# Moving one transpose and one store to other queues, reordering the early loads, and folding in smaller steps in a matmul-bound kernel

## The chip, the cores and the metric

One core of one Trainium2 chip. The time is device microseconds of one execution, the median over runs; all runs told here are of the state fast. The profile's span is some 1.8 us shorter than the time of the same run (567.7 beside 569.45 before the change).

## The reference, cut to what matters

```python
B, N, C = 4, 5824, 256
qn = q / (norm(q, axis=1) + 1e-6);  kn = k / (norm(k, axis=1) + 1e-6)
a  = softmax(kn^T @ qn / tau)              # 256 x 256 per batch
x  = (v @ a).reshape(B * N, C)
out = ((x @ w1) * (x @ w2)) @ w3 @ w_out   # d_ff = 1024
```

The kernel never forms x. It folds the softmax into w1 and w2 per batch (`Wf`), multiplies v transposed (`vT`) by it, and forms W = w3 @ w_out once.

## The kernel before

Three places matter. The first folds, 256 columns of each half at a time, with the eviction cut in two:

```python
def first_folds():
    sum_mm(0)
    for c1 in range(CT): quarter_mm(0, c1, 0)      # 2 matmuls of 256 columns
    sum_mm(1)
    for c1 in range(CT): quarter_mm(0, c1, 1)      # then Wf by ScalarE (c1 = 0) and VectorE
```

The start of the main loop: w3 is loaded right behind v pieces 1 and 2; piece 1 of v is transposed on TensorE, piece 2 by DMA behind the transposes of w3; loads for the next batch follow. `hold` is a one-element GpSimd copy that reads what a transpose wrote, so GpSimd issues nothing further until it has landed:

```python
load_piece("v", 0, 1); load_piece("v", 0, 2)
nc.gpsimd.dma_start(out=wout_sb, ...); nc.gpsimd.dma_start(out=w3_bf, in_=w3r)
# ... (cut)
at(7.0, 0.5, lambda: transpose_half_on_pe(0, 1, 0, True))
at(8.0, 0.5, lambda: transpose_half_on_pe(0, 1, 1, False))
at(15.0, 0.0, transpose_w3)
at(15.0, 0.0, lambda: transpose_piece(0, 2))
for jt in range(FT):
    at(27.5 + 1.2 * jt, 0.87, lambda jt=jt: w_unit(jt))     # the products w3 @ w_out
moves = [("qk", 1, 0, 29.0), ("v", 0, 3, 30.0), ("v", 0, 4, 30.5), ("qk", 1, 1, 44.0), ...]
```

The last stores: two of 64 left rows each on SyncE, one of 128 rows on ScalarE's queue:

```python
for m in (b - 1, b):
    nc.sync.dma_start(out=out[m * N + NT * P : (m + 1) * N, :], in_=o2[k : k + LEFT, :])
```

Of the kernel before, what the change touches and what calls it, by code (L numbers as in the profile page):

```python
# [12 lines left out]
F32 = DT.float32  # L13
BF16 = DT.bfloat16

P = 128
# [9 lines left out]
def kernel(  # L26
# [113 lines left out]
    def transpose_half_on_pe(n, pi, h, on_act):  # L140
        if pi == 0 and h == 0:
            new_vT(n)
        t = pieces["v", n, pi]
        i0 = 4 * h
        pe_transpose(
            vTs[n][0][:, pi * PIECE + i0 : pi * PIECE + i0 + 4, :, :].rearrange("p i c t -> p (i c) t"),
            [t[:, i0 + i, ct * P : (ct + 1) * P] for i in range(4) for ct in range(CT)],
            "out", on_act,
        )
# [93 lines left out]
    def soft_units(n):  # L243
# [133 lines left out]
            for c2 in range(CT):  # L377
                fold_mm((w, c1, h * 512, (h + 1) * 512), c2, tag, i % 2 == 0 or (n == 0 and i == 7))

        def quarter_mm(lo, c1, c2):  # L380

            if c2 == 0:
                tag = "ab" if lo == 0 else "out"
                st[lo, c1] = psum.tile(
                    [P, 2, 256], F32, tag=tag, name=f"quarter_{lo}_{c1}", bufs={"ab": 4, "out": 3}[tag]
                )
            m = st[lo, c1]
            for w in range(2):
                nc.tensor.matmul(  # L389
                    m[:, w, :], lhsT=st["e"][:, c2, c1 * P : (c1 + 1) * P], rhs=w12[:, c2, w, lo : lo + 256],  # L390
                    start=(c2 == 0 and w == 0), stop=(c2 == CT - 1 and w == 1), skip_group_check=True,
                )
            if c2 == CT - 1:
                for o in (0, P) if lo == 0 else (slice(0, 256),):
                    cols = slice(o, o + P) if lo == 0 else o
                    dst, src = Wf[n][:, c1, :, lo : lo + 256][:, :, cols], m[:, :, cols]
                    if c1 == 0:
                        nc.scalar.activation(out=dst, in_=src, func=AF.Copy, scale=st["rs"][:, c1 : c1 + 1])  # L398
                    else:
                        nc.vector.tensor_scalar_mul(dst, src, st["rs"][:, c1 : c1 + 1])  # L400

        def first_folds():
            sum_mm(0)
            for c1 in range(CT):
                quarter_mm(0, c1, 0)
            sum_mm(1)
            for c1 in range(CT):
                quarter_mm(0, c1, 1)

        def second_quarter():  # L410
            for c1 in range(CT):
                for c2 in range(CT):
                    quarter_mm(256, c1, c2)

        if n == 0:
            return [k_first, k_row, q_first, scaled_first, first_folds, second_quarter, sum_start] + [lambda i=i: fold(i) for i in range(4, 8)]
# [24 lines left out]
    def at(t, cost, fn):  # L441
        seq[0] += 1
        agenda.append((t, seq[0], cost, fn))
# [22 lines left out]
    def hold(src):  # L466

        nc.gpsimd.tensor_copy(gate_t, src)  # L468
# [33 lines left out]
    def emit_out(b, c, j, ab, only=None):  # L502

        small = c == NCH - 1
        if small:
            lhs = [ab[:, :P]]
            if b % 2 == 1:
                lhs.append(lefts[b // 2][:, j, :, :].rearrange("p b t -> p (b t)")[:, P : P + 2 * LEFT])
        else:
            lhs = [ab[:, i * P : (i + 1) * P] for i in range(4)]  # L510
        if j == 0:
            out_tiles[b, c] = [
                psum.tile([P, 2, D], F32, tag="out", name=f"o_{b}_{c}_{h}", bufs=3)
                for h in range(len(lhs) if small else 2)
            ]
        tl = out_tiles[b, c]
        for s, lhsT in reversed(list(enumerate(lhs))) if small else enumerate(lhs):
            if only is not None and s != only:
                continue
            h, o = (s, 0) if small else divmod(s, 2)  # L520
            nc.tensor.matmul(  # L521
                tl[h][:, o, :], lhsT=lhsT, rhs=W_sb[:, j, :],
                start=(j == 0 and o == 0), stop=(j == FT - 1 and (small or o == 1)),
                skip_group_check=True,
            )
        clock[0] += len(lhs) * (D * MM_COL + MM_FIX)
        if j == FT - 1:
            o = work.tile([P, 4, D], F32, tag="o_sb", name=f"osb_{b}_{c}", bufs=3)
            rows = out[b * N : b * N + NT * P, :].rearrange("(p i) c -> p i c", i=NT)
            if small:  # L530
                if b % 2 == 1 and only != 0:
                    o2 = work.tile([P, D], F32, tag="kr", name=f"oleft_{b}", bufs=1)
                    nc.vector.tensor_copy(o2, tl[1][:, 0, :])
                    for m in (b - 1, b):
                        k = (m - b + 1) * LEFT
                        nc.sync.dma_start(out=out[m * N + NT * P : (m + 1) * N, :], in_=o2[k : k + LEFT, :])
                if only != 1:
                    nc.scalar.copy(o[:, 0, :], tl[0][:, 0, :])
                    other = nc.scalar if b == B - 1 else nc.sync
                    other.dma_start(out=rows[:, NT - 1, :], in_=o[:, 0, :])  # L540
            else:
                nc.scalar.copy(o[:, 0:2, :], tl[0])  # L542
                nc.vector.tensor_copy(o[:, 2:4, :], tl[1])  # L543
                nc.sync.dma_start(out=rows[:, 4 * c : 4 * c + 4, :], in_=o)
            if only is None:
                del out_tiles[b, c]
# [72 lines left out]
    load_part("v", 0, 0, half, PIECE)  # L619
    load_piece("v", 0, 1)  # L620
    load_piece("v", 0, 2)
    nc.gpsimd.dma_start(out=wout_sb, in_=moe_w_out.rearrange("(lh ll) c -> ll lh c", ll=P))
    nc.gpsimd.dma_start(out=w3_bf, in_=w3r)
    squares("k", 4, whole)
    for sl in (lo, hi):
        squares("q", 4, sl)
# [19 lines left out]
    def w_unit(jt):  # L646
# [10 lines left out]
        if jt == FT - 1:  # L657
            w_ready[0] = True

    def load_library():  # L660

        m = work.tile([P, 1], F32, tag="lib", name="lib", bufs=1)
        nc.gpsimd.partition_all_reduce(m, ones_f, P, ReduceOp.add)


    def make_agenda(b):
        agenda.clear()
        clock[0] = 0.0
        n = b + 1
        if b == 0:  # L670
            at(0.5, 0.87, soft0[5])
            for i in range(4):
                at((1.7, 2.6, 3.5, 3.9)[i], 0.43, soft0[7 + i])
            at(0.0, 0.0, load_library)
            at(4.6, 0.5, lambda: transpose_half_on_pe(0, 0, 1, False))
            at(7.0, 0.5, lambda: transpose_half_on_pe(0, 1, 0, True))
            at(8.0, 0.5, lambda: transpose_half_on_pe(0, 1, 1, False))
            at(15.0, 0.0, transpose_w3)
            at(15.0, 0.0, lambda: transpose_piece(0, 2))
            for jt in range(FT):  # L680
                at(27.5 + 1.2 * jt, 0.87, lambda jt=jt: w_unit(jt))
            moves = [("qk", 1, 0, 29.0), ("v", 0, 3, 30.0), ("v", 0, 4, 30.5), ("qk", 1, 1, 44.0), ("qk", 1, 2, 45.0)]
            moves += [("qk", 1, 3, 53.0), ("qk", 1, 4, 55.0), ("v", 0, 5, 61.0), ("qk", 1, 5, 73.0)]
            moves += [("v", 1, 0, 88.0), ("v", 1, 1, 98.0), ("v", 1, 2, 120.0), ("qk", 2, 0, 130.0)]
            t0, t1 = 54.0, 113.0
        else:
            moves = [("v", b, 3, 1.0), ("qk", n, 1, 10.0), ("qk", n, 2, 17.0), ("v", b, 4, 26.0), ("qk", n, 3, 38.0)]
            moves += [("v", b, 5, 46.0), ("qk", n, 4, 58.0), ("qk", n, 5, 66.0)]
            moves += [("v", n, 0, 76.0), ("v", n, 1, 86.0), ("v", n, 2, 96.0), ("qk", n + 1, 0, 108.0)]
            moves = [m for m in moves if m[1] < B]  # L690
            t0, t1 = 16.0, 98.0

        before = (0, 2) if b == 0 else None
        for nm, m, pi, t in moves:
            if before is not None and not (nm == "v" and before == (m, pi - 1) == (0, 3)):
                at(t, 0.0, lambda w=before: hold(vTs[w[0]][1][:1, 0, :1] if w[1] == NP_ - 1 else vTs[w[0]][0][:1, w[1] * PIECE, 0, :1]))
            at(t, 0.0, gate)
            if nm == "qk":
                at(t, 0.0, lambda m=m, pi=pi: load_qk(m, pi))
                before = None  # L700
            else:
                at(t, 0.0, lambda m=m, pi=pi: load_piece("v", m, pi))
                at(t + 4.0, 0.0, lambda m=m, pi=pi: transpose_piece(m, pi))
                before = (m, pi)
        if n == B:
            agenda.sort()
            return
        units = score_units(n)
        for i, (cst, fn) in enumerate(units):
            at(t0 + (t1 - t0) * i / len(units), cst, fn)  # L710
        soft = soft_units(n)
        for cst, t, fn in soft:
            at(t1 + 1.0 + t, cst, fn)
        agenda.sort()
# [55 lines left out]
```

## Time and profile before

| | before |
|---|---|
| median (lowest to highest) | 569.44 us (569.25 to 569.69) |
| first main matmul (a) starts | 37.27 us |
| last matmul starts | 563.39 us |
| gaps between matmuls after the first a | 1.13 us |
| last store lands / span ends | 566.76 / 567.68 us |

A gap is read from the starts of consecutive matmuls: what a step exceeds 0.216 us after 512 columns, 0.109 after 256, 0.082 after 192 and 0.055 after 128 by, where that is over 0.03 us. The three parts of the table, head, matmuls with their gaps, and tail, add up to the span.

### The profile page before, as it was taken

Reading aid. Unit: us, or ns where it says so; the run is one execution under the profiler, and the core shown is the slowest. Engines: PE = TensorE matmul, PEld = TensorE weight load, DVE = VectorE, ACT = ScalarE, POOL = GpSimd, SP = SyncE. Lnnn points to the kernel's source line nnn. Section 1 sums busy time; section 2 is a strip of 40 time slices with the busy share of each in tenths; the row PEclk is TensorE's granted clock in tenths of the full one; section 3 lists DMA queues with packets and bytes.
Section 4 is the critical chain, followed back from the end, with each engine's and each line's share of the span. In section 5 each row is a group of like instructions: output and inputs, shape, how many; then the busy total and the mean of one; then the engine's idle time right before and its main releaser. Section 6 shows DMA issues by size and latency. Waiting matters only on the chain.

```text
span 567.7 us, 10095 instructions
## 1 busy us (share of the span) xinstructions
PE 557.6 (98%) x3755; PEld 355.4 (63%) x3755; DVE 375.4 (66%) x581; ACT 338.7 (60%) x627; POOL 77.9 (14%) x163
## 2 busy tenths in 40 slices
PE   8799999999999999999999999999999999999997
PEld 5664566776656666666656566666655655665655
DVE  1047645888966577888766668787876665565564
ACT  1057536777766577777675567777765554454453
POOL 4260013120111111121210101030120000000000
PEclk9999999999999999999999999999999999999999
DMA  9999989978455796595661595765740325221011
GB/s 213 211 182 209 173 171 237 226 164 192 115 142 121 143 192 148 90 193 123 145 149 75 97 219 117 155 120 121 185 112 39 85 74 149 64 68 71 38 70 61
DMA packets 75104, 77.45 MB, mean 136 GB/s; under 512 B 54192, under 2 KB 58800, under 8 KB 75056
## 3 DMA queue, kind: packets, MB, share of 16 engines
q0 software_dynamic: 15760, 38.93, 39.3%
q1 hardware_dynamic: 59008, 37.23, 22.0%
q10 hardware_dynamic: 288, 0.66, 0.4%
q8 instruction: 29, 0.48, 0.3%
q14 instruction: 19, 0.16, 0.1%
HBM read 78.91 MB, written 23.86 MB: 181 GB/s over the span
## 4 chain that ended last, share of the span: by engine, by line
PE 93%; DMA 5%; ACT 1%; POOL 0%; issue 0%; DVE 0%; ACTq 0%; POOLq 0%
PE o L521 28%; PE b L476 28%; PE a L476 28%; PE G L192 5%; DMA k<-in_k_dram 5%; PE fold L363 2%; PE w L649 1%; ACT kr L283 0%; PE quarter L389 0%; POOL k L111 0%; POOL q L111 0%; PE sqk L225 0%; PE row L271 0%; ACT e L322 0%; ACT Wf L398 0%
## 5 line engine op out<-in xcount | busy, mean ns | idle before, releaser
L497 DVE TENSOR_TENSOR abs<-as,b 128x512 bf16<-128x512 bf16 x336 | 230.6, 687 | 143.9 <-ACT as L482 131.4
L482 ACT CAST as<-a 128x512 bf16<-128x512 f32 (+1 forms) x384 | 215.9, 562 | 170.4 <-DVE abs L497 84.7
L476 PEld LDWEIGHTS <-Wf 128*128 128x128 bf16 x1536 | 149.0, 98 | 102.3 <-ACT Wf L398 0.6
L476 PE MATMUL a<-vT,Wf 128*128 128x512 bf16 x704 | 209.6, 379 | 0.4 <-ACT Wf L398 0.4
L476 PE MATMUL b<-vT,Wf 128*128 128x512 bf16 x704 | 209.6, 379 | 0.0
L521 PE MATMUL o<-W_sb,abs 128*128 128x256 bf16 x1344 | 201.5, 273 | 0.0
L521 PEld LDWEIGHTS <-abs 128*128 128x128 bf16 x1344 | 131.2, 98 | 79.8 <-issue 0.2
L201 DVE TENSOR_TENSOR acc<-acc,sq 128x1024 f32<-128x1024 f32 x66 | 80.4, 1219 | 0.6 <-ACT sq L189 0.6
L192 PE MATMUL G<-k,q 128*128 128x256 bf16 x276 | 49.8, 273 | 0.0
L189 ACT ACTIVATE sq<-q 128x512 f32<-128x512 bf16 x66 | 41.8, 633 | 0.0
L189 ACT ACTIVATE sq<-k 128x512 f32<-128x512 bf16 x66 | 41.5, 629 | 0.0
L464 POOL COPY gate_t<-abs 1x1 bf16<-1x1 bf16 x39 | 10.5, 269 | 171.7 <-DVE abs L497 168.8
L543 DVE COPY osb<-o 128x512 f32<-128x512 f32 x44 | 30.1, 685 | 0.9 <-PE o L521 0.9
L192 PEld LDWEIGHTS <-q 128*128 128x128 bf16 x276 | 27.0, 98 | 3.1
L542 ACT COPY osb<-o 128x512 f32<-128x512 f32 x44 | 25.8, 586 | 4.1 <-PE o L521 2.1
L468 POOL COPY gate_t<-vT 1x1 bf16<-1x1 bf16 x16 | 3.1, 193 | 158.8 <-DMA vT<-v 158.8
L111 POOL DMA_DIRECT2D q<-in_q_dram x28 | 15.1, 540 | 12.5 <-DMA k<-in_k_dram 5.5
L370 ACT ACTIVATE Wf<-fold,rs 128x512 bf16<-128x512 f32 x15 | 10.3, 687 | 10.9 <-PE fold L363 8.7
L283 ACT ACTIVATE kr<-row 128x256 f32<-128x256 f32 x1 | 0.4, 383 | 26.1 <-PE row L271 26.1
L363 PE MATMUL fold<-w,e 128*128 128x512 bf16 x56 | 15.0, 379 | 0.0
L487 DVE TENSOR_TENSOR left<-as,b 128x192 bf16<-128x192 bf16 x32 | 11.3, 354 | 5.1 <-ACT as L482 2.7
L497 DVE TENSOR_TENSOR abq<-as,b 128x512 bf16<-128x512 bf16 x16 | 10.8, 686 | 5.0 <-ACT as L482 4.5
(98 smaller groups left out, 242.3 us busy)
## 6 DMA issues: line engine op xcount, KB each, us to landing
out_dram<-osb SPq DMA_DIRECT2D x44, 512.0 KB, 3.3
k<-in_k_dram POOLq DMA_DIRECT2D x19, 512.0 KB, 8.3
v<-in_v_dram POOLq DMA_DIRECT2D x19, 512.0 KB, 5.2
q<-in_q_dram POOLq DMA_DIRECT2D x18, 512.0 KB, 5.8
w_wout<-in_moe_w_dram POOLq DMA_DIRECT2D x1, 2048.0 KB, 22.7
k<-in_k_dram POOLq DMA_DIRECT2D x4, 320.0 KB, 8.8
v<-in_v_dram POOLq DMA_DIRECT2D x4, 320.0 KB, 4.9
q<-in_q_dram POOLq DMA_DIRECT2D x3, 320.0 KB, 4.1
```

What stands on the lines that cost most here:

```text
L111: nc.gpsimd.dma_start(out=pieces[nm, n, pi][:, lo:hi, :], in_=qk_main[nm, n][0][:, pi * PIECE + lo : pi * PIECE + hi, :])
L189: nc.scalar.activation(out=dst[:, :, part, :], in_=src[:, o : o + 2, :], func=AF.Square)
L192: nc.tensor.matmul(G[:, ct, :], lhsT=qt[:, i, ct * P : (ct + 1) * P], rhs=kt[:, i, :], start=(pr == 0 and part == 0 and ct == 0), stop=(pr ...
L201: nc.vector.tensor_add(accs[n], accs[n], sqs[0])
L363: nc.tensor.matmul(m, lhsT=st["e"][:, c2, c1 * P : (c1 + 1) * P], rhs=w12[:, c2, w, lo:hi], start=(c2 == 0), stop=(c2 == CT - 1),)
L476: nc.tensor.matmul(t[:, :n], lhsT=Wf[b][:, ct, w, j * P : (j + 1) * P], rhs=rhs_of(b, c, ct), start=(ct == 0), stop=(ct == CT - 1),)
L482: nc.scalar.copy(a_sb[:, :n], tiles[0][:, :n])
L487: nc.vector.tensor_mul(both, a_sb[:, :n], tiles[1][:, :n])
L497: nc.vector.tensor_mul(ab, a_sb, tiles[1])
L521: nc.tensor.matmul(tl[h][:, o, :], lhsT=lhsT, rhs=W_sb[:, j, :], start=(j == 0 and o == 0), stop=(j == FT - 1 and (small or o == 1)), skip ...
L542: nc.scalar.copy(o[:, 0:2, :], tl[0])
L543: nc.vector.tensor_copy(o[:, 2:4, :], tl[1])
```

## The change

Its intent: take sixteen transposes off TensorE, start the first fold's eviction sooner, keep the transfer queue free for what is needed first, and let the last two stores start side by side.

```diff
+            for c1 in range(CT):                      # first folds: 128 + 128 columns
+                for c2 in range(CT):
+                    columns_mm(P, P, c1, c2)
-                        nc.sync.dma_start(out=..., in_=o2[k : k + LEFT, :])
+                        eng = nc.gpsimd if m == B - 1 else nc.sync
+                        eng.dma_start(out=..., in_=o2[k : k + LEFT, :])
-    nc.gpsimd.dma_start(out=wout_sb, ...)             # behind the v loads
-    nc.gpsimd.dma_start(out=w3_bf, in_=w3r)
-            at(7.0, 0.5, lambda: transpose_half_on_pe(0, 1, 0, True))
-            at(8.0, 0.5, lambda: transpose_half_on_pe(0, 1, 1, False))
+            at(0.0, 0.0, lambda: transpose_piece(0, 2))
+            at(0.0, 0.0, lambda: transpose_piece(0, 1))
+            at(0.0, 0.0, lambda: hold(vTs[0][0][:1, PIECE, 0, :1]))
+            at(0.0, 0.0, load_w3)                     # the two loads above
-                at(27.5 + 1.2 * jt, 0.87, lambda jt=jt: w_unit(jt))
+                at(35.5 + 1.2 * jt, 0.87, lambda jt=jt: w_unit(jt))
-            moves = [("qk", 1, 0, 29.0), ("v", 0, 3, 30.0), ("v", 0, 4, 30.5), ("qk", 1, 1, 44.0), ...]
+            moves = [("qk", 1, 0, 35.0), ("v", 0, 3, 35.5), ("qk", 1, 1, 49.0), ..., ("v", 0, 4, 60.0), ...]
```

(Cut: the rest of the moves, renamings, and the first hold, which now waits for the last transpose of w3.)

More of the change, by code (lines that the diff above doesn't have):

```diff
@@ L378, in fold, with columns_mm @@
                 fold_mm((w, c1, h * 512, (h + 1) * 512), c2, tag, i % 2 == 0 or (n == 0 and i == 7))
-        def quarter_mm(lo, c1, c2):
+        def columns_mm(lo, width, c1, c2):
             if c2 == 0:
-                tag = "ab" if lo == 0 else "out"
+                tag = "ab" if lo < 256 else "out"
                 st[lo, c1] = psum.tile(
-                    [P, 2, 256], F32, tag=tag, name=f"quarter_{lo}_{c1}", bufs={"ab": 4, "out": 3}[tag]
+                    [P, 2, width], F32, tag=tag, name=f"columns_{lo}_{c1}", bufs={"ab": 4, "out": 3}[tag]
                 )
@@ L389, in quarter_mm @@
                 nc.tensor.matmul(
-                    m[:, w, :], lhsT=st["e"][:, c2, c1 * P : (c1 + 1) * P], rhs=w12[:, c2, w, lo : lo + 256],
+                    m[:, w, :], lhsT=st["e"][:, c2, c1 * P : (c1 + 1) * P], rhs=w12[:, c2, w, lo : lo + width],
                     start=(c2 == 0 and w == 0), stop=(c2 == CT - 1 and w == 1), skip_group_check=True,
@@ L393, in quarter_mm @@
             if c2 == CT - 1:
-                for o in (0, P) if lo == 0 else (slice(0, 256),):
-                    cols = slice(o, o + P) if lo == 0 else o
-                    dst, src = Wf[n][:, c1, :, lo : lo + 256][:, :, cols], m[:, :, cols]
-                    if c1 == 0:
-                        nc.scalar.activation(out=dst, in_=src, func=AF.Copy, scale=st["rs"][:, c1 : c1 + 1])
-                    else:
-                        nc.vector.tensor_scalar_mul(dst, src, st["rs"][:, c1 : c1 + 1])
+                dst = Wf[n][:, c1, :, lo : lo + width]
+                if c1 == 0:
+                    nc.scalar.activation(out=dst, in_=m, func=AF.Copy, scale=st["rs"][:, c1 : c1 + 1])
+                else:
+                    nc.vector.tensor_scalar_mul(dst, m, st["rs"][:, c1 : c1 + 1])
         def first_folds():
@@ L404, in first_folds @@
             for c1 in range(CT):
-                quarter_mm(0, c1, 0)
+                columns_mm(0, P, c1, 0)
             sum_mm(1)
             for c1 in range(CT):
-                quarter_mm(0, c1, 1)
+                columns_mm(0, P, c1, 1)
+            for c1 in range(CT):
+                for c2 in range(CT):
+                    columns_mm(P, P, c1, c2)
         def second_quarter():
@@ L412, in second_quarter @@
                 for c2 in range(CT):
-                    quarter_mm(256, c1, c2)
+                    columns_mm(256, 256, c1, c2)
         if n == 0:
@@ L535, in emit_out @@
                         k = (m - b + 1) * LEFT
-                        nc.sync.dma_start(out=out[m * N + NT * P : (m + 1) * N, :], in_=o2[k : k + LEFT, :])
+                        eng = nc.gpsimd if m == B - 1 else nc.sync
+                        eng.dma_start(out=out[m * N + NT * P : (m + 1) * N, :], in_=o2[k : k + LEFT, :])
                 if only != 1:
@@ L621 @@
     load_piece("v", 0, 2)
-    nc.gpsimd.dma_start(out=wout_sb, in_=moe_w_out.rearrange("(lh ll) c -> ll lh c", ll=P))
-    nc.gpsimd.dma_start(out=w3_bf, in_=w3r)
     squares("k", 4, whole)
@@ L658, in w_unit, with load_w3 @@
             w_ready[0] = True
+    def load_w3():
+        nc.gpsimd.dma_start(out=wout_sb, in_=moe_w_out.rearrange("(lh ll) c -> ll lh c", ll=P))
+        nc.gpsimd.dma_start(out=w3_bf, in_=w3r)
     def load_library():
@@ L675, in make_agenda @@
             at(4.6, 0.5, lambda: transpose_half_on_pe(0, 0, 1, False))
-            at(7.0, 0.5, lambda: transpose_half_on_pe(0, 1, 0, True))
-            at(8.0, 0.5, lambda: transpose_half_on_pe(0, 1, 1, False))
-            at(15.0, 0.0, transpose_w3)
-            at(15.0, 0.0, lambda: transpose_piece(0, 2))
+            at(0.0, 0.0, lambda: transpose_piece(0, 2))
+            at(0.0, 0.0, lambda: transpose_piece(0, 1))
+            at(0.0, 0.0, lambda: hold(vTs[0][0][:1, PIECE, 0, :1]))
+            at(0.0, 0.0, load_w3)
+            at(16.0, 0.0, transpose_w3)
             for jt in range(FT):
-                at(27.5 + 1.2 * jt, 0.87, lambda jt=jt: w_unit(jt))
-            moves = [("qk", 1, 0, 29.0), ("v", 0, 3, 30.0), ("v", 0, 4, 30.5), ("qk", 1, 1, 44.0), ("qk", 1, 2, 45.0)]
-            moves += [("qk", 1, 3, 53.0), ("qk", 1, 4, 55.0), ("v", 0, 5, 61.0), ("qk", 1, 5, 73.0)]
-            moves += [("v", 1, 0, 88.0), ("v", 1, 1, 98.0), ("v", 1, 2, 120.0), ("qk", 2, 0, 130.0)]
+                at(35.5 + 1.2 * jt, 0.87, lambda jt=jt: w_unit(jt))
+            moves = [("qk", 1, 0, 35.0), ("v", 0, 3, 35.5), ("qk", 1, 1, 49.0), ("qk", 1, 2, 51.0), ("qk", 1, 3, 55.0)]
+            moves += [("qk", 1, 4, 57.0), ("v", 0, 4, 60.0), ("qk", 1, 5, 80.0), ("v", 0, 5, 83.0)]
+            moves += [("v", 1, 0, 97.0), ("v", 1, 1, 106.0), ("v", 1, 2, 120.0), ("qk", 2, 0, 130.0)]
             t0, t1 = 54.0, 113.0
@@ L691, in make_agenda @@
             t0, t1 = 16.0, 98.0
-        before = (0, 2) if b == 0 else None
+        before = "w3" if b == 0 else None
         for nm, m, pi, t in moves:
             if before is not None and not (nm == "v" and before == (m, pi - 1) == (0, 3)):
-                at(t, 0.0, lambda w=before: hold(vTs[w[0]][1][:1, 0, :1] if w[1] == NP_ - 1 else vTs[w[0]][0][:1, w[1] * PIECE, 0, :1]))
+                at(t, 0.0, lambda w=before: hold(w3T[-1][:1, 1, FT - 1, :1] if w == "w3" else vTs[w[0]][1][:1, 0, :1] if w[1] == NP_ - 1 else vTs[w[0]][0][:1, w[1] * PIECE, 0, :1]))
             at(t, 0.0, gate)
```

## The prediction

> **What bounds the kernel now.** I read the page first: which engine is full, and the chain of work that ended last.
>
> ```profile
> PE 557.6 (98%) x3755; PEld 355.4 (63%) x3755; DVE 375.4 (66%) x581; ACT 338.7 (60%) x627; POOL 77.9 (14%) x163
> ...
> PE   8799999999999999999999999999999999999997
> ...
> DMA  9999989978455796595661595765740325221011
> ...
> PE 93%; DMA 5%; ACT 1%; POOL 0%; issue 0%; DVE 0%; ACTq 0%; POOLq 0%
> ```
>
> TensorE is busy in every slice but the first two and the last, and 93% of the chain is matmuls. A busy PE need not be at its peak, so I also took the starts of all 3755 matmuls from the trace: from the first a product (37.27 us) on, the step to the next start is 0.216 us for 512 columns, 0.109 for 256 and 0.055 for 128 nearly without exception; everything above those steps adds up to 1.1 us in 526 us. So the time is three terms: the head until the first a product, the matmul columns after it, and the tail. Outside head and tail, only fewer columns help, and only a new stall hurts.
>
> The head, from the chain of waits between 30 and 48 us (start, length, what):
>
> ```profile
> 15.74 14.71 DMA k<-in_k_dram
> ...
> 35.18 0.52 ACT e L322
> 35.70 0.05 issue
> 35.75 0.20 PE sum L340 x2
> 35.95 0.46 PE quarter L389 x4
> 36.41 0.04 PE sum L340 x2
> 36.45 0.02 issue
> 36.47 0.18 DVE rs L348
> ...
> 36.74 0.48 ACT Wf L398
> 37.22 0.05 issue
> 37.27 0.60 PE a L476 x2
> ```
>
> The last k piece sets 30.45 us, then a softmax chain leads to the first half of Wf on ScalarE. The tail, from the timeline of the last microseconds:
>
> ```profile
> 563.48 0.42 DVE L533 COPY oleft<-o 128x256 f32<-128x256 f32 x1 [0.55 <-PE o L521]
> 563.70 0.37 ACT L538 COPY osb<-o 128x256 f32<-128x256 f32 x1 [1.16 <-PE o L521]
> 563.93 1.13 SPq L536 DMA_DIRECT2D out_dram<-oleft  x2
> 564.10 0.36 ACTq L540 DMA_DIRECT2D out_dram<-osb  x1
> ```
>
> The trace's landings of these three stores are 566.25 (first left rows), 566.59 (the ACT store) and 566.76 us (second left rows); the span ends 0.92 us after the last.
>
> Third, the transfers of the first 160 us, which the change reorders. The load of w3 is issued behind the v pieces; the views of issues and of waits say:
>
> ```profile
> w_wout<-in_moe_w_dram POOLq DMA_DIRECT2D x1, 2048.0 KB, 22.7
> ```
> ```profile
> POOL gate_t L468 <- DMA vT<-v: 49.8, 2, 34.8
> ```
>
> 22.7 us from issue to landing, and GpSimd holds the loads of the next batch for 34.8 us until the DMA transposes are through. In the single records: v piece 2 lands at 46.85, wout at 49.51, w3 at 59.40; its four transposes, issued from 59.49, land at 63.83, 65.59, 69.52 and 71.11; the first w product starts at 65.59 and needs them.
>
> **What the Trainium skill says.** "TensorE: Matmul & The Clock Gate", section "Wait — 56ns, not 53.3ns?", gives N / 2.4 GHz + about 2.5 ns from start to start of warm matmuls, 55.6 ns at 128 columns; the trace agrees (55.3 ns in the PE transposes). The section "Back-to-back issue gap" there puts a stream with weight loads at some 81 ns per matmul of 128 columns; this trace does not show that: eight transposes with their eight weight loads take 0.45 us. "DMA: Bandwidth & Descriptors", section "DMA Transpose (X-bar)", binds the plain DMA transpose to the Sync and Scalar queues, so here it shares SyncE's order with w3's transposes and the output; the trace has all of them on that queue. The same page, "Anatomy of one DMA — SWDGE (gpsimd) path", gives some 2.0 us of fixed time plus the movement; the trace is near it: an undisturbed 512 KB v load takes 5.0 us, of which 2.45 us is its movement (the spacing of landings in a full queue).
>
> **The change part by part.** The order of the built program was compared too: 3744 matmuls in place of 3752.
>
> 1. Second v piece. Two groups of eight PE transposes go: 16 x 0.0553 = 0.885 us of PE time, which lies wholly on the path, plus two evictions (1.01 us of ScalarE, 0.69 us of VectorE) that do not. In their place stands one DMA transpose, behind that of piece 2. Both wait for v piece 2 at 46.85; an undisturbed transpose lands 3.65 us after its issue, a second in a row 1.8 us later, so piece 1 is there at about 52.5. Laying the new PE order out with the steps above, chunk 2 starts at 54.1 us: hidden, by 1.5 us. Net -0.89 us.
>
> 2. First folds by 128 columns. Matmul columns are the same. The a product waits for ScalarE's Wf, which waits for the reciprocal, which waits for the second sum; that one is bound by e, done at 36.09, and its weight load (36.14 to 36.24), not by the fold between them. The second 128 columns (8 x 0.055 = 0.44 us) fall into the wait for ScalarE from 36.5 to 37.2. VectorE's half starts some 0.2 us sooner but was not waited for. Net 0 to -0.1; I take -0.03.
>
> 3. w3 behind the transposes. The load is held until piece 1 is transposed (52.5, plus 0.5 for the hold). With 5.2 us for wout and 9.9 us more for w3 (59.40 - 49.51) it lands at 68.2, and its transposes by the pattern above at 72.6, 74.4, 78.3 and 79.9. The w products move from 27.5 to 35.5 on the schedule clock that the kernel keeps while it is built; in the layout they start at 73.1 (first), 76.6, 79.2 and 81.8 (first of each later pair). Margins 0.5, 2.2, 0.9 and 1.9 us, from 1.8, 2.6, 1.3 and 2.3 before. While w is missing, outputs are put off: 42 units where buffers hold 50, so no stall from that.
>
> 4. Late v behind q and k. The first loads of batch 1 wait for the last w3 transpose: q at 80.3, then k, v piece 3 landing at 90.3 (10 us, as from 73.73 to 83.79 now); its transpose lands at 94.0, chunk 6 needs it at 94.6. Only then come q and k piece 1 (94.4, landing at 99.7 and 102.3, as 91.70 gave 96.99 and 99.55); the score product that needs them is at 102.2. Then v 4 and its transpose, near 126 against 128.3; v 5; v 0 and 1 of batch 1; near 154 GpSimd comes to the all-reduce of batch 1's norms, which starts at 153.81 now with about 1 us of slack in the chain behind it. This is one serial row of transfers with little slack at each stop. Because a stall at one stop also delays PE at all later ones, what counts is the largest lateness, not the sum. By these estimates it is about 0.1 us at the k piece and 0 to 1 us at the all-reduce; an error of 1 us anywhere in the row is a stall of about as much. I book +0.4 us.
>
> 5. Last left rows by two queues. The second store can start at 563.9, not 564.48; but the ACT store lands at 566.59 anyway, 0.17 us before today's last. If GpSimd's store takes 2.4 to 2.9 us it lands at 566.3 to 566.8. Net -0.17 to +0.1; I take -0.1.
>
> Sum: -0.89 - 0.03 + 0.4 - 0.1 = -0.62 us; 569.44 - 0.62 = 568.8 us.
>
> **The rivals.** (a) All new transfers are hidden: the stall term is 0, giving 568.4, or 568.2 if the tail gains its full 0.17 and the folds 0.1. For it: the schedule numbers were visibly chosen with care, PE hardly stalls today, every stop comes out within a microsecond. (b) The serial row is late: w3 starts some 17 us later than it could (wout flows right behind v piece 2 today, but now waits for a transpose, a hold and a new issue), and each hold adds a round trip in which the queues stand still. 1.5 to 3 us of stall would give 570 to 571.5. For it: the margins of 0.5 us; and the two queues share engines (a store issued at 98.92 landed at 107.81 beside the loads). Against it: the new order has no transfers beside each other where I assumed none. (c) The head gains: if w3's traffic slowed the end of the head, moving it would help more. Against it: w3 is issued at 36.69, after the last k (30.45), and its queue works in order. Worth 0. (d) The GpSimd store costs more at the end than estimated: up to +0.5 us.
>
> **Range and chances.** Without a stall 568.2 to 568.5; a moderate one 568.8 to 569.5; the late row above 570. I put 0.35, 0.45 and 0.2 on these. Predicted 568.8, range 568.0 to 570.3. Two per cent is 11.4 us; nothing in the change is that large in either direction: faster 0.01, within 0.98, slower 0.01.
>
> **What would show it right or wrong.** Step 1: 16 matmuls fewer on the PE transposes, chunk 2's first a product without idle PE before it. Step 2: the first a product at 37.2. Step 3: w3 landing near 68 and no gap before the first w product at 73. Step 4: no idle PE before chunk 6, the first score product of piece 1, chunk 8 and the sums of batch 1 near 167; a gap there, put down to a DMA or to ScalarE, is rival (b), and its length is the error. Step 5: the three last landings within 0.3 us of each other. The prediction fails if one of those gaps exceeds 1.5 us, or if the last landing comes more than 3.3 us after the last eviction starts.

## The result, and the profile after

The changed kernel takes 575.10 us (574.43 to 576.75, 5 runs), against 569.44. The ratio is 1.0106 (95% interval 1.0091 to 1.0122). Ratios here are the mean time of one kernel's fast runs over that of the other's fast runs of the same rounds, so not quite the ratio of the medians. The profiled run is the slowest of the five (576.75), so its stalls are on the large side.

The page's chain, as shown of before:

```profile
PE 74%; issue 13%; DMA 10%; POOL 1%; ACT 1%; DVE 0%; POOLq 0%; DVEq 0%
```

"issue", time in which the engine at the chain's end waited for nothing the profile shows, was 0% and is 13%. The chain of the last 31 us alone says where that is:

```profile
494.24 71.29 issue
565.53 0.59 POOLq L770
```

The chain no longer ends in matmuls. It ends on the sequencer of GpSimd (POOLq), in the line that closes the program. The 71 us of "issue" are not a loss of 71 us: GpSimd was idle then and TensorE worked. They only lead back from the end of the program to GpSimd's work before its last store. The timeline of the end shows nothing after 566.1 us, though the span ends at 574.98:

```profile
564.84 0.42 DVE L534 COPY oleft<-o 128x256 f32<-128x256 f32 x1 [0.55 <-PE o L522]
565.06 0.37 ACT L540 COPY osb<-o 128x256 f32<-128x256 f32 x1 [1.16 <-PE o L522]
565.29 0.49 SPq L538 DMA_DIRECT2D out_dram<-oleft  x1
565.46 0.36 ACTq L542 DMA_DIRECT2D out_dram<-osb  x1
565.56 0.56 POOL L538 DMA_DIRECT2D out_dram<-oleft  x1 [71.32 <-DVE oleft L534]
```

The three stores land at 567.65, 567.99 and 568.15 us. What fills the other 6.8 us is an instruction that neither the timeline nor the busy times count. It belongs to the line that closes the program; asked for by that line, the trace gives it (duration in ns min/median/max, first and last start). First the changed kernel, then the kernel before, in a window around 492 us:

```profile
L770 POOLq DRAIN  x3: 52/102/8656, 565.5 to 574.7; - x3
```
```profile
L765 POOLq DRAIN  x1: 8672/8672/8672, 492.2 to 492.2; - x1
```

GpSimd's program ends with a DRAIN of 8.66 us. Before the change GpSimd had its last work at 492 us, and the same DRAIN, 8.67 us, ran under the matmuls. It was in the trace all along, and hidden. Now GpSimd's last work is the last store, and the program cannot end before 565.53 + 8.66 = 574.19.

The rest of the difference is in the matmuls. The waits between 70 and 110 us (waiting line, releaser, us, times, longest):

```profile
PEld L649 <- DMA w3T<-w_wout: 1.8, 1, 1.8
PE w L649 <- DMA w3T<-w_wout: 1.3, 1, 1.3
...
PE G L192 <- DMA k<-in_k_dram: 0.7, 1, 0.7
...
PEld L477 <- DMA vT<-v: 0.3, 1, 0.3
```

And the chain in the same stretch, cut to the transfers (start, us, what):

```profile
70.56 3.85 DMA w3T<-w_wout
...
82.56 9.89 DMA v<-in_v_dram
92.45 0.02 issue
92.46 3.69 DMA vT<-v
...
97.52 7.15 DMA k<-in_k_dram
104.66 0.04 issue
104.71 0.38 PE G L192 x2
```

Nothing of the kind stood there before: TensorE now waits for a row of transfers at three of the stops the prediction listed. The span, taken apart by the profiled runs:

| | before | after | difference |
|---|---|---|---|
| first a starts | 37.27 | 36.98 | -0.29 |
| matmul steps fewer (16 x 0.0553) | | | -0.89 |
| gaps after the first a | 1.13 | 3.61 | +2.48 |
| last matmul starts (measured) | 563.39 | 564.75 | +1.36 |
| from there to the end of the span | 4.29 | 10.23 | +5.94 |
| span | 567.68 | 574.98 | +7.30 |

The first three rows give +1.30, the matmul end +1.36; the rest is rounding. The new gaps are 1.47 us before the first w product, 0.22 before chunk 6 and 0.90 before the first score product of k piece 1.

### The profile page after: what moved, and what is told of

Same layout as the page of the kernel before. It is cut to its first block, busy times and chain, and to the rows that moved or that the text cites. A ratio compares the mean times of both kernels' runs of the same rounds, so it can differ in the third digit from the quotient of the medians.

```text
span 575.0 us, 10086 instructions
## 1 busy us (share of the span) xinstructions
PE 556.3 (97%) x3747; PEld 354.2 (62%) x3747; DVE 375.0 (65%) x580; ACT 338.5 (59%) x626; POOL 79.9 (14%) x166
## 4 chain that ended last, share of the span: by engine, by line
PE 74%; issue 13%; DMA 10%; POOL 1%; ACT 1%; DVE 0%; POOLq 0%; DVEq 0%
PE a L477 22%; PE b L477 22%; PE o L522 22%; DMA k<-in_k_dram 6%; PE G L192 5%; PE fold L363 2%; DMA v<-in_v_dram 2%; DMA w3T<-w_wout 1%; DMA vT<-v 1%; DVE abs L498 0%; POOL q L111 0%; POOL k L111 0%; ACT kr L283 0%; PE columns L389 0%; PE w L649 0%
## 5 line engine op out<-in xcount | busy, mean ns | idle before, releaser
L469 POOL COPY gate_t<-vT 1x1 bf16<-1x1 bf16 x17 | 4.4, 259 | 167.3 <-DMA vT<-v 167.3
L111 POOL DMA_DIRECT2D q<-in_q_dram x28 | 15.2, 541 | 12.5 <-DMA k<-in_k_dram 5.3
L111 POOL DMA_DIRECT2D v<-in_v_dram x25 | 13.5, 544 | 4.4 <-issue 3.3
```

What stands on the lines that cost most here:

```text
L111: nc.gpsimd.dma_start(out=pieces[nm, n, pi][:, lo:hi, :], in_=qk_main[nm, n][0][:, pi * PIECE + lo : pi * PIECE + hi, :])
```

## The experiments

All were correct. The median of "before" in the same rounds was 569.2 to 569.5 us each time.

**Part 5 undone, or alone.** First (e1), the changed kernel with both left stores on SyncE again:

```diff
-                        eng = nc.gpsimd if m == B - 1 else nc.sync
+                        eng = nc.sync
```

> The changed kernel with part 5 undone: both last left stores on SyncE again. Theory A (a DRAIN of 8.66 us closes GpSimd's program after its last DMA; it ends the span when that DMA is the last work): the last landing is again followed by about 0.9 us, the time falls by about 5.9 us to about 569.2, and the stalls before the first w product and the first score product of piece 1 stay (some 2.4 us together). Rival B (the late transfer row costs the whole loss): the time stays near 575.

570.17 us (569.18 to 570.76), ratio 1.0011 (0.9996 to 1.0026). The span ends 1.33 us after the last landing; I had expected about 0.9, as before the change. So the loss from 1.0106 is nearly all gone, but the kernel is not faster than before either, and its spread (1.6 us) is some three times as wide. Its profiled run is its fastest and has only 0.15 us of gap at the k piece and none before w: there w3 landed at 68.76 us, in the changed kernel's profiled run at 70.48.

The 0.4 us more at the end have a cause of their own. SyncE's program closes with a row of nine waits, most of them for transfers, some 0.06 us each, then short DRAINs (the first of these starts at the first time shown). First e1, then the kernel before:

```profile
L770 SPq DRAIN  x3: 7/7/7, 566.6 to 566.9; - x3
```
```profile
L765 SPq DRAIN  x3: 7/7/13, 566.8 to 567.2; - x3
```

The last stores had landed at 566.08 and 566.76, so SyncE was through its row 0.5 us after the landing in e1 and 0.1 us after it before. In the single records the wait for the last store stands second of the nine in e1 and last before; in e1 the other seven come after the landing. All five kernels with piece 1's transpose by DMA and no store on GpSimd at the end (e1, e5, e6, e9, e10) end 1.33 to 1.35 us after the last landing, and those with TensorE's transposes and no late work on GpSimd (before, e4, e7, e8) 0.90 to 0.98. In the changed kernel itself the row runs under the DRAIN. That the one transfer more on SyncE shifts the order of the row is likely, but no run tests it.

Then (e2) the kernel before with that store alone on GpSimd:

```diff
-                        nc.sync.dma_start(out=..., in_=o2[k : k + LEFT, :])
+                        eng = nc.gpsimd if m == B - 1 else nc.sync
+                        eng.dma_start(out=..., in_=o2[k : k + LEFT, :])
```

> The kernel before with part 5 alone. Theory A: DRAIN from about 563.9 to 572.6, span about 573.4, time 575.2 (+5.7). Rival C (the store itself lands late through the software path): the span ends about 0.9 us after a landing that lies several us later than 566.8.

575.54 us, ratio 1.0106 (1.0089 to 1.0123): the whole loss of the change, by part 5 alone. The store itself was not late, it landed at 567.14, 2.6 us after its issue. The closing line of its trace, read as above:

```profile
L766 POOLq DRAIN  x3: 52/102/8659, 564.5 to 573.7; - x3
```

**How the DRAIN behaves.** The kernel before with another store on GpSimd, once the last full chunk (e3), once the one ahead of it (e4):

```diff
-                nc.sync.dma_start(out=rows[:, 4 * c : 4 * c + 4, :], in_=o)
+                eng = nc.gpsimd if (b, c) == (B - 1, 10) else nc.sync      # (B - 1, 9) in the second
+                eng.dma_start(out=rows[:, 4 * c : 4 * c + 4, :], in_=o)
```

> The kernel before with its last full output chunk (512 KB, issued at 561.56 on SyncE) issued by GpSimd instead. Theory A with a DRAIN of fixed length: DRAIN from about 561.5 to 570.2, span about 571.0, time 572.7 (+3.3). Rival D (the DRAIN's length follows the bytes of the last store, here eight times as many): longer than 8.7 us, time 575 or more.

> The kernel before with the output chunk ahead of that (512 KB, issued at 551.57) issued by GpSimd. Theory A: the DRAIN ends near 560.3, before the last stores, and costs nothing: time 569.4 within 0.3. Rival C (any store through the software path costs): slower by over 1 us.

573.27 us, ratio 1.0071, and 569.50 us, ratio 1.0001 (0.9986 to 1.0016). The closing lines of the two traces, e3 first:

```profile
L766 POOLq DRAIN  x3: 52/93/8636, 562.0 to 571.2; - x3
```
```profile
L766 POOLq DRAIN  x3: 52/93/9392, 552.3 to 567.7; - x3
```

Eight times the bytes of the left store leave the length at 8.64 us; it is 9.39 us in the other. The cost follows the moment of GpSimd's last work: 6.0 us at 564.5 (569.43 x 0.0106), 4.0 at 562.0 (569.43 x 0.0071), nothing at 552.3, where the DRAIN ends at 561.7, under the last stores.

Is it the DMA that makes the DRAIN long, or only that GpSimd ends late? The kernel before with a one-element GpSimd copy as the last thing of the program, no store (e11):

```diff
         emit_out(*pend[i], only=only)
+    gate()          # nc.gpsimd.tensor_copy(gate_t, last_ab[0][:1, :1])
```

> The kernel before with a one-element copy on GpSimd as its last instruction (after the last a*b product, near 563), no store on GpSimd. Theory A1 (the closing DRAIN is long only soon after a software DMA): DRAIN of about 0.1 us, time 569.4 within 0.3. Theory A2 (the closing DRAIN takes 8.66 us whenever GpSimd's program ends): DRAIN from about 563 to 571.8, time 574 (+4.5).

573.82 us, ratio 1.0078. GpSimd's last DMA had been issued 70 us earlier, and still the closing line reads:

```profile
L766 POOLq DRAIN  x3: 46/93/8204, 563.1 to 571.8; - x3
```

So my first reading, that a software DMA brings the DRAIN with it, was too narrow. The DRAIN closes GpSimd's program in all thirteen traces; near the end of the program it costs time, behind a copy of one element as much as behind a store. Why it takes 8 to 9 us is not shown by these runs. All of them use GpSimd's all-reduce as well, so whether a program without it has the long DRAIN is open.

**The transfer row.** First (e5), e1 with the w products 1 us later. More does not fit: with 2 us or more a simulation ahead of the run stopped in a deadlock, so part 3 already stands at the edge of what the deferred products can be kept in.

```diff
-                at(35.5 + 1.2 * jt, 0.87, lambda jt=jt: w_unit(jt))
+                at(36.5 + 1.2 * jt, 0.87, lambda jt=jt: w_unit(jt))
```

> The changed kernel with both left stores on SyncE (as e1) and the w products 1 us later in the schedule (36.5 in place of 35.5; more does not fit the buffers). Theory E (one serial row of transfers, where the largest lateness counts): the gap before the first w product goes, but the one before the first score product of piece 1 grows by what PE no longer loses before it; the time stays at e1's 570.2 within 0.4. Rival F (each gap is lost on its own): up to 1 us faster than e1, 569.2.

570.42 us (569.14 to 572.16), ratio 1.0017 (1.0002 to 1.0033), as e1 within the noise. In its profiled run w3 was as late as in the changed kernel's (69.94 against 70.48), the gap before w was 0.11 us in place of 1.47, but chunk 6 now waited 1.73 us in place of 0.22, and the k piece 0.23 in place of 0.90: 2.07 us together, against 2.59; with a further gap of 0.43 us near 167 us, behind VectorE, it is 2.50. TensorE's timeline of this run at chunk 6's first product, with the wait before it in brackets:

```profile
95.20 0.59 PE L477 MATMUL a<-vT,Wf 128*128 128x512 bf16 x2 [1.57 <-DMA vT<-v]
```

The gap went to the next stop of the row. That agrees with theory E: one serial row, of which the largest lateness counts.

Then the hold itself was taken away, so that w3 flows behind v piece 2 as it did before (e6):

```diff
-            at(0.0, 0.0, lambda: hold(vTs[0][0][:1, PIECE, 0, :1]))
             at(0.0, 0.0, load_w3)
```

> As e1, but the hold ahead of the load of w3 is taken out, so that w3 flows right behind v piece 2 and beside the transposes of pieces 2 and 1, as it did before the change. Theory E: w3 lands at 60 to 62, every stop of the row comes some 6 to 8 us sooner, no gap before the first w product, chunk 6 or the first score product of piece 1: 568.4 (568.1 to 568.8), about 1 us faster than before and 1.7 us faster than e1, with a spread as small as that of before. Rival G (part 1 itself or other loads cost, not the hold): 569.4 or more.

A clear miss: 580.78 us, ratio 1.0199. w3 did land at 60.88, as expected. But now the transposes were late. The same line in this kernel and in the changed one (duration of the issue in ns min/median/max):

```profile
L157 SPq DMA_TRANSPOSE vT<-v x2: 4086/7404/10723, 47.0 to 57.8; - x2
```
```profile
L157 SPq DMA_TRANSPOSE vT<-v x2: 1726/1956/2186, 47.1 to 48.8; - x2
```

The first transpose was issued at 47.03 in both. Beside the load of w3 its issue alone took 10.7 us, and it landed at 62.21, after w3, in place of 51.13. The queues of that stretch (47 to 62 us; packets, MB, share) say how the engines were divided:

```profile
q0 software_dynamic: 1511, 2.33, 85.6%
q1 hardware_dynamic: 2627, 0.66, 33.0%
```

A transpose moves in packets of 0.66 MB / 2627, about 250 bytes, the load in packets of 1540. The Trainium skill ("DMA: Bandwidth & Descriptors", section "Queues, rings and completion order") has each DMA engine take turns between its queues packet by packet; if the packets that the profile counts are those, a transpose with packets of a sixth of the size moves slowly for as long as a load flows. While w3's load flowed (49.7 to 60.6 us) 1251 packets of the transposes went beside 877 of the load, 0.32 MB beside 1.76. The run agrees in kind, though not packet for packet; it does not prove it. Chunk 2 waits for the second transpose, landed at 64.00, and then runs slowly for a while (stretch, its length, busy time of PE, PEld, DVE, ACT and POOL with counts, then the granted clock, the DMA share and GB/s):

```profile
54.00:64.00 10.00, 0.40 (x2) 0.00 (x0) 1.13 (x2) 0.58 (x1) 0.00 (x0) 0.70 1.20 211
64.00:68.00 4.00, 3.96 (x10) 1.48 (x11) 0.94 (x2) 1.17 (x2) 0.00 (x0) 0.50 1.18 263
68.00:72.00 4.00, 4.00 (x20) 1.74 (x19) 2.82 (x5) 2.42 (x5) 0.03 (x1) 0.97 0.98 215
```

The gap is 9.81 us, and for the next 4 us the granted clock is 0.50: steps of 0.426 us in place of 0.216, 2.0 us more. This is the clock gate of the skill's "TensorE: Matmul & The Clock Gate", section "What's actually happening", which halves the clock after an idle window of about 3.4 us and restores it after as long a busy one; the trace agrees (the clock fell some 3.8 us into the idle time and was back 4.3 us after TensorE restarted). The changed kernel's gaps, 1.5 us at most, are shorter, and its granted clock stays at 1.00 in the 4 us after each.

So the hold is not a mistake; it is what part 1 costs. With part 1 undone as well (e7, PE transposes, w3 not held):

```diff
+            at(7.0, 0.5, lambda: transpose_half_on_pe(0, 1, 0, True))
+            at(8.0, 0.5, lambda: transpose_half_on_pe(0, 1, 1, False))
-            at(0.0, 0.0, lambda: transpose_piece(0, 1))
```

> As e6, with part 1 undone: piece 1 of v by sixteen PE transposes again. 0.885 us more PE time on the path: 569.3 (0.7 to 1.1 us slower than e6). If the transposes were hidden by something else: the same as e6.

569.83 us (569.48 to 569.88), ratio 1.0004 (0.9992 to 1.0016), and no gap at any transfer. Against e6 this is 11 us faster and not 0.9 slower: my expectation hung on e6's and fell with it. Piece 2's transpose also crept here (issue 10.8 us, landed at 61.73), but only chunk 4 needs it.

Last, e1 with the two transposes in the order in which their pieces land, and the hold on the later one (e9); and the same with the second left store behind ScalarE's own, on its queue (e10, whose further edit issues that store there):

```diff
-            at(0.0, 0.0, lambda: transpose_piece(0, 2))
             at(0.0, 0.0, lambda: transpose_piece(0, 1))
-            at(0.0, 0.0, lambda: hold(vTs[0][0][:1, PIECE, 0, :1]))
+            at(0.0, 0.0, lambda: transpose_piece(0, 2))
+            at(0.0, 0.0, lambda: hold(vTs[0][0][:1, 2 * PIECE, 0, :1]))
```

> As e1, with the transpose of piece 1 ahead of that of piece 2 (piece 1's load lands 2.45 us sooner), and the hold on piece 2's. Theory E: the first transpose starts at 44.7 beside the load of piece 2, the second lands near 51.5 in place of 52.5, so w3 and the whole row come about 1 us sooner; the gaps of e1 shrink by up to 1 us: 569.2 (568.5 to 569.6), 0.5 to 1 us faster than e1's 570.2. Rival F (the gaps do not hang on the hold): as e1.

> As e9, with the second of the last left stores on ScalarE's queue behind its own store, that is the intent of part 5 without GpSimd. Theory A: no long DRAIN at the end; landings within 0.2 us of today's, the time as e9 within 0.3.

568.81 us (568.77 to 569.86), ratio 0.9989 (0.9977 to 1.0002), and 569.14 us (568.66 to 569.40), ratio 0.9990 (0.9976 to 1.0003). Both medians are below that of before (569.45), by 0.3 to 0.6 us, but the intervals just reach 1: probably faster, not shown. They are about 0.002 (1.2 us) below e1's ratio; theory E had 0.5 to 1 us. Both still pay the 0.4 us of SyncE's closing row. In the second one's trace the later transpose landed at 51.19 (52.51 in e1), w3 at 67.52, and no gap was left at w, chunk 6 or the k piece. The profiled run of the first is its slowest; there the loads ahead came late (piece 1 at 46.11, 44.32 in e1), the transposes landed no sooner (52.78), and 0.63 us of gap stood at the k piece and 0.41 us at a fold. So that the earlier hold makes the gain is seen in e10's trace, not in e9's. The store on ScalarE's queue landed at 566.14, 0.19 us after the store before it, and the span ended 1.35 us later, with the long DRAIN at 491.6 us, under the matmuls: harmless, and not to be told from a gain of 0.

**Part 2 alone** (e8), the kernel before with the first folds of the change (`columns_mm` and `first_folds` as in the diff above):

> The kernel before with part 2 alone. By the prediction 0 to 0.1 us faster: 569.35, not to be told from 569.44 by the times; in the trace, the time from the start of e to the first a product, 2.09 us now, becomes 1.99 to 2.09.

569.25 us, ratio 0.9996 (0.9984 to 1.0009). The trace tells what the times can't; from e8's timeline:

```profile
34.96 0.91 ACT L322 ACTIVATE e<-s,r 128x256 bf16<-128x256 f32 x2 [0.44 <-DVE r L309]
...
36.42 0.84 ACT L396 ACTIVATE Wf<-columns,rs 128x256 bf16<-128x256 f32 x2 [0.56 <-PE columns L389]
...
36.95 0.61 PE L477 MATMUL a<-vT,Wf 128*128 128x512 bf16 x2
```

From the start of e to the first a product it is 36.95 - 34.96 = 1.99 us; before it was 37.27 - 35.18 = 2.09. Part 2 gains 0.1 us: this time is 1.99 to 2.00 us in all eight traces with the new folds and 2.08 to 2.09 in the five without. The rest of the head's 0.29 us in the changed kernel is e starting 0.2 us sooner (34.98). That is scatter: e starts between 34.96 and 35.64 us in the thirteen traces, with and without the change.

## Why the prediction was wrong

It said 568.8 us, 568.0 to 570.3; measured were 575.10. Point by point:

- **Step 5 failed, in the sentence "the span ends 0.92 us after the last" landing**, carried over from the kernel before. The store was sized rightly: 2.59 us from issue to landing against 2.4 to 2.9, last landing 0.16 us after ScalarE's. But the end of the program also waits for GpSimd's closing DRAIN of 8.66 us. Its cost measured alone is +6.0 us (569.43 x 0.0106) where I had -0.1. It could have been found blind: the trace of before holds it at 492 us. I looked only at busy instructions and landings, and never at when each engine's own program ended. Rival (d) named the right place but allowed 0.5 us. The list of what would prove me wrong looked at gaps and landings, and neither of its signs came: the longest gap was 1.47 us (limit 1.5), and the last landing came 3.1 us after the last eviction started (limit 3.3).
- **Step 4's size was off**: +0.4 us booked for stalls. The profiled run has 2.6 us; on average it is less. Without the DRAIN the kernel is at ratio 1.0011, some 0.6 us slower than before (569.4 x 0.0011). Without a stall it should be 0.5 faster (0.9 from the matmuls, less the 0.4 of SyncE's closing row, which I did not foresee either), so my estimate is about 1.1 us of stall (the interval of e1 leaves 0.2 to 1.9). Which rival that is: (b), the late row; the profiled run lies in its 1.5 to 3 us, the average below them.
- **Step 3's term for w3** is what was mis-sized first: landing at 70.48 (68.76 to 69.94 in e1, e5 and e9) where I worked out 68.2 (my own terms add up to 68.1). wout took 5.6 to 6.3 us and not 5.2, and w3 after it 10.0 to 11.6 and not 9.9. The margin of 0.5 us at the first w product went with that. At chunk 6 the next loads weighed more: w3's last transpose was only 0.6 us late (80.49 against 79.9), but q, k and v piece 3 behind it took 11.1 us (81.35 to 92.45) where I had copied 10 from one trace. Rival (b)'s cause, the holds and round trips, agrees with the waits, and "largest lateness, not the sum" with the gap that moved from w to chunk 6.
- **Step 1 was right**: piece 1 was there at 52.86 (52.5 predicted), no gap before chunk 2, 16 matmul steps gone. I did not see that the hold is its price: I counted the lateness of w3 as a thing by itself, when taking the hold away makes the transposes unusable (e6).
- **Step 2 was right**: 0.10 us, at the edge of 0 to 0.1.
- **Rival (a)** is nearly what the repaired kernels reach (568.8 and 569.1 against 568.4; SyncE's closing row is 0.4 of the difference); **rival (c)**, a gain in the head from moving w3, is not seen: e8, which leaves w3 where it was, has the same early start of e.

## What to carry to other kernels

Before moving work to an engine that has been idle at the end, look at how that engine's program closes: an engine's last instruction sets when its closing work starts, and what was hidden under other engines becomes the tail, as the 8.66 us here. Read a transfer schedule as one row with a need at each stop; in e5 delaying a consumer only moved the gap to the next stop, and starting the row sooner (e9, e10) is the likely repair. A DMA transpose landed 4.1 us after its issue alone and 15.2 beside a load (e6); where it must be there soon, count what has to wait meanwhile into its price.

## What the Trainium skill lacked or had wrong

- No page has GpSimd's long closing DRAIN. "VectorE: DVE Perf Modes", section "The DRAIN you can't avoid", gives the closing DRAINs as constantly some 12 ns on all five engines; here GpSimd's longest one takes 8.20 to 9.39 us in all thirteen traces, after a DMA or a one-element copy alike.
- "DMA: Bandwidth & Descriptors", section "DMA Transpose (X-bar)", says nothing of a transpose beside a plain load: its issue went from 1.7 to 10.7 us and its landing from 4.1 to 15.2 us after the issue while the load of w3 flowed.
- "TensorE: Matmul & The Clock Gate", section "Back-to-back issue gap", has some 81 ns per matmul of 128 columns with weight loads and 131 ns for 512; here 55 ns and 216 ns hold in streams in which every matmul has its own weight load.
